# Phase A's last 768 tokens as a Strassen pair of halves in a kernel of attention and two gated MLPs

## The chip, the cores and the metric

One core of a Trainium2 chip runs the whole kernel. The metric is the device time of one execution in microseconds (us); lower is better. Several runs give a median, and one more execution is profiled.

## The reference, cut to what matters

Attention with a window of 32 positions (plain in four heads, with a step of 4 in the other four) runs over 4 sequences of 576 positions and 8 heads of 64. Its output, 2304 tokens by 512, goes through two MLPs one after the other.

```
x = attention(q, k, v)                      # 2304 tokens x 512
# phase A: d_ff 1536
a = x @ w_a;  b = x @ w_b
x1 = (a * b) @ w_out
# phase B: d_ff 2048
h = x1 @ w_in
g = maximum(h, 0) + alpha * minimum(h, 0)
out = g @ w_out2
```

## The kernel before

The weights come as float64, and their words are turned on the chip into float32 (`float_of`: two ScalarE operations, two VectorE operations for a block of 128x512). Every float32 operand of a matmul is then split into a high and a low part (`split`: a copy to fp32r gives the high part, a subtraction the low one), and each product is three matmuls: high by high, high by low, low by high (`mm3`). The contraction runs over features, tokens are the moving columns.

Two large SBUF tensors, `rt` (fp32r) and `ft` (float32), are cut by hand into places and rings that are used again over the phases. The program is recorded in steps: `step` records one block of 12 matmuls, then lets each conversion on the `belt` go one stage further, then whatever was asked for with `at_step`. A scheduler then sets the order on each engine, so a step's place is only the order in which things were written down. All DMAs go out from SyncE's one queue (SP), in its order, and an instruction there that waits holds back those behind it.

Phase A goes over tokens in `TILES`: 512, 512, 512, 256 and 512. For each of 12 blocks f of 128 features a tile does 12 matmuls into `pa` (w_a), 12 into `pb` (w_b), multiplies the two, splits the product, and does 12 matmuls into the four banks `accA` (w_out). So a tile has 432 matmuls of the tile's width. Beside tile 0 the weights w_a, w_b (`in_wab`) and w_out (`in_wo`) are loaded and converted; w_out's parts are written to DRAM (`wod`) and loaded again for each later tile through `wo_ring`, which has two places. Beside tiles 0 to 2 the attention of the next sequence runs; the tiles 3 and 4 have none.

Phase B goes over three pairs of 384 tokens, and does h by Strassen's scheme (Winograd's form): tokens in two halves, features in two halves, seven products in place of eight. One group is two feature blocks, seven `product`s of 6 matmuls of 384 columns (L593), and between them slots for `task`s, each 12 matmuls into `accB`, with the splits of earlier gates. The seven weight factors of each group are formed by `convert_s` beside tiles 1 to 4, written to DRAM (`wsd`) and loaded through `ws_ring`, which has seven places. The 16 blocks of w_out2 (`w2o`) are converted from `start_of[4] + 21` on, one every 3.5 steps, so most of them beside phase B's first groups.

The lines that matter are L389 to L391 (the three matmuls of `mm3`), L593 (`product`), L262 (reload of `wod`), L505 (load of `wsd`), L182 (load of raw weights), L164 to L174 (`float_of`), L232 and L235 (`split`), L404, L405 (`split_x` at the turn of a tile), L496, L497 (`split_x1`, the seven inputs of the products), L658 and L604 (copies and additions that put Strassen's sums together).

Of the kernel before, what the change touches and what calls it, by code (L numbers as in the profile page):

```python
# [33 lines left out]
TILES = [(0, 512), (512, 512), (1024, 512), (1536, 256), (1792, 512)]  # L34

HT = 384
# [23 lines left out]
def tile_kernel(ctx: ExitStack, tc: tile.TileContext, qk, v, mask, wab, wo1, w2, alpha, out):  # L60
# [6 lines left out]
    wod = dram.tile([NFA, 128, 1024], F32, name="wod")  # L67
    wsd = dram.tile([NFB // 2, 7, 128, 512], F32, name="wsd")
# [33 lines left out]
    raw_b_ring = Ring(ft, 4096, 1024, 2)  # L102
# [9 lines left out]
    mk = cut(ft, a0 + 4648, 720).bitcast(BF16).rearrange("p (m k) -> p m k", m=5)  # L112

    xs = [cut(rt, 4096 + 1536 * i, 2, 2, HT) for i in range(7)]
    w2o = [cut(rt, 16384 + 1024 * f if f < 12 else 1024 * (f - 12), 2, 512) for f in range(NFB)]
    gq_ring = Ring(rt, 28672, 2 * HT, 3)
    ws_ring = Ring(rt, 30976, 512, 7)
    ws_ring.places = ws_ring.places[3:] + ws_ring.places[:3]
# [120 lines left out]
    def job_w(k, f, j):  # L239
# [5 lines left out]
        queue.append((k, convert(wab[f, j], dest)))  # L245

    def job_o(k, f):
# [4 lines left out]
        def then():  # L252
            nc.sync.dma_start(out=wod[f], in_=wo[0, f].rearrange("p h n -> p (h n)").bitcast(F32))
# [257 lines left out]
    start_of = [n_start + 3 * NFA * t + t for t in range(n_tiles + 1)]  # L511
    for t in range(1, n_tiles):
        for f in range(NFA):
            reload_o(start_of[t] + 3 * f, t, f)
    for t in range(3):
        lag = (1, 2, 3, 4, 6)
        for i in range(NC * NG):
            Group(t + 1, i, start_of[t] + int(i * 2.64), lag, steady)
# [12 lines left out]
    def first_sums():  # L531
        srcs[0] = sums_x1()

    k = start_of[4]
    at_step(after, k + 2, begin_b)
    at_step(after, k + 8, first_sums)
    for j in range(7):
        at_step(after, k + 20 + 2 * j, lambda j=j: split_x1(j, srcs[0][j]))
    for j in range(7):
        at_step(after, k + 3 * NFA, lambda j=j: load_ws(j))  # L540
# [14 lines left out]
    for t, (t0, n) in enumerate(TILES):  # L555
        assert now[0] == start_of[t], (now[0], start_of[t])
        if t < 3:
            xn[t + 2] = cut(ft, 2048 * (t % 2), 4, 512)
        for f in range(NFA):
# [15 lines left out]
            if final and t + 1 < n_tiles:  # L575
# [11 lines left out]

    def product(i, acc, start):
        w, x = loaded.pop(0), xs[i]
# [15 lines left out]


    tasks = [(p, h, f) for p in range(NP) for h in range(2) for f in range(NFB)]
    ready, split_of, out_accs = {}, {}, []
    n_split = [0]

    def prepare():

        while n_split[0] < len(tasks) and len(split_of) < 3 and tasks[n_split[0]] in ready:
            task = tasks[n_split[0]]
            n_split[0] += 1
            g = ready.pop(task)
            q = gq_ring.next().rearrange("p (h n) -> p h n", h=2)
            split(q[:, 0], q[:, 1], g, nc.scalar, nc.vector)
            split_of[task] = q
            g_free.append(g)  # L620

    def task():
        if not tasks or tasks[0] not in split_of:
            return
        n_split[0] -= 1
        p, h, f = it = tasks.pop(0)
        q = split_of.pop(it)
        if f == 0:
            out_accs[:] = new_accs(f"B{p}{h}")
        expand(out_accs, w2o[f][:, 0], w2o[f][:, 1], q, HT, f == 0, f == NFB - 1)  # L630
        if f == NFB - 1:
            t0 = (2 * p + h) * HT
            for c in range(NC):
                def evacuate_b(acc=out_accs[c], c=c, t0=t0):
                    ev = ev_ring.next()
                    if c % 2:
                        nc.vector.tensor_copy(ev, acc[:, :HT])
                    else:
                        nc.scalar.copy(ev, acc[:, :HT])  # L639
                    nc.sync.dma_start(out=out[c, :, t0:t0 + HT], in_=ev)  # L640
                at_step(after, now[0], evacuate_b)

    def bslot(products=None, *then):

        for fn in then:
            at_step(after, now[0], fn)
        at_step(after, now[0], prepare)
        step(products)

    def group(p, i):  # L650
        f0, f1 = 2 * i, 2 * i + 1
        last = i == NFB // 2 - 1
        b0, b1, b2 = (ps.tile([128, 512], F32, tag=t, bufs=n, name=t) for t, n in (("at", 2), ("pa", 1), ("pb", 1)))
        s1, s2, s3 = s_places
        if (p, i) == (0, 7):
            g_free.extend(g_late)
        c11, c12, c21, c22 = (g_free.pop(0) for _ in range(4))
        copy = lambda out, acc: nc.scalar.copy(out, acc[:, :HT])  # L658

        def run(j, acc, start):  # L660
            def products():
                product(j, acc, start)
# [7 lines left out]
        bslot(run(0, b0, True), lambda: copy(s1, b0), lambda: refill(0))  # L670
# [78 lines left out]
```

## Time and profile before

| | us |
|---|---|
| median of 3 runs | 945.01 (943.8 to 948.72) |
| the profiled execution | 949.16 |
| its span, first to last instruction | 947.4 |
| PE busy in the span | 929.5 (98%) |
| VectorE (DVE), ScalarE (ACT), GpSimd (POOL) busy | 537.7, 385.7, 64.8 |

Matmuls are pipelined and their ends are modelled, so PE's busy time says where it had work, not that it was at its peak. Where PE runs without a wait, the time of a stretch divided by the matmuls that started in it is what one costs.

### The profile page before, as it was taken

The numbers are of one execution on the slowest core, as the hardware profiler recorded it, in microseconds if no ns is written. First come the engines' busy times: TensorE is split into PE (matmuls) and PEld (weight loads), VectorE is DVE, ScalarE is ACT, GpSimd is POOL, SyncE is SP. The second block draws the span as 40 slices with busy tenths as digits, with TensorE's granted clock in tenths as the row PEclk, the third lists the DMA queues.
The fourth block names the chain that finished last, engine by engine and source line by source line (L and its number), as shares of the span: only waits on it lengthen the run. The fifth ranks groups of instructions, "written<-read, shape, count | busy, mean of one in ns | idle before, by whom it ended". The sixth has DMA issues, their size and how long they took to land.

```text
span 947.4 us, 15065 instructions
## 1 busy us (share of the span) xinstructions
PE 929.5 (98%) x5641; PEld 811.2 (86%) x5644; DVE 537.7 (57%) x1116; ACT 385.7 (41%) x908; POOL 64.8 (7%) x70
## 2 busy tenths in 40 slices
PE   8899999999999999999999999899999999999997
PEld 5577777777787777799888879899999999999997
DVE  5689986534445353453524349868746485546442
ACT  5588884523344343433522336524222242222221
POOL 0000000200203030303500000000000000000000
PEclk9799999999999999999999999999999999999999
DMA  7568863534436343477735358756545435344200
GB/s 206 167 221 290 284 232 134 195 126 161 151 121 221 125 173 99 159 280 250 245 130 177 109 174 315 246 152 196 175 119 150 122 112 156 112 140 134 72 34 34
DMA packets 71401, 158.65 MB, mean 167 GB/s; under 512 B 8097, under 2 KB 22689, under 8 KB 71329
## 3 DMA queue, kind: packets, MB, share of 16 engines
q1 hardware_dynamic: 71328, 157.70, 50.8%
q8 instruction: 45, 0.74, 0.3%
q14 instruction: 28, 0.22, 0.1%
HBM read 127.25 MB, written 30.41 MB: 166 GB/s over the span
## 4 chain that ended last, share of the span: by engine, by line
PE 89%; DMA 5%; DVE 2%; ACT 1%; issue 1%; SPq 1%; POOL 0%; ACTq 0%; DVEq 0%; POOLq 0%
PE at L593 7%; PE accB L391 6%; PE accB L390 6%; PE accB L389 6%; PE accA L389 5%; PE pa L389 5%; PE pb L389 5%; PE accA L390 5%; PE accA L391 5%; PE pb L391 5%; PE pa L391 5%; PE pb L390 5%; PE pa L390 5%; PE pb L593 4%; PE pa L593 4%; PE sp L306 3%
## 5 line engine op out<-in xcount | busy, mean ns | idle before, releaser
L232 ACT CAST rt<-ft 128x512 fp32r<-128x512 f32 (+2 forms) x240 | 132.1, 558 | 279.6 <-PE accB L391 168.9
L235 DVE TENSOR_TENSOR rt<-ft,rt 128x512 fp32r<-128x512 f32 (+2 forms) x208 | 129.9, 626 | 128.1 <-ACT rt L232 126.4
L390 PE MATMUL accB<-rt 128*128 128x384 f32 x384 | 128.4, 334 | 0.0
L391 PE MATMUL accB<-rt 128*128 128x384 f32 x384 | 128.0, 334 | 0.0
L389 PE MATMUL accB<-rt 128*128 128x384 f32 x384 | 125.8, 334 | 0.4 <-ACT ft L639 0.4
L593 PE MATMUL at<-rt 128*128 128x384 f32 x432 | 89.0, 336 | 3.8 <-DMA rt<-wsd 2.7
L389 PE MATMUL accA<-rt 128*128 128x512 f32 (+1 forms) x240 | 91.2, 383 | 1.2 <-DMA rt<-wod 1.2
L389 PE MATMUL pa<-rt 128*128 128x512 f32 (+1 forms) x236 | 90.9, 385 | 0.5 <-ACT rt L404 0.4
L389 PE MATMUL pb<-rt 128*128 128x512 f32 (+1 forms) x236 | 90.0, 381 | 0.0
L572 DVE TENSOR_TENSOR ft<-ft,pb 128x512 f32<-128x512 f32 (+1 forms) x59 | 37.2, 630 | 92.6 <-PE pb L391 84.9
L390 PE MATMUL pa<-rt 128*128 128x512 f32 (+1 forms) x236 | 87.8, 372 | 1.2 <-DVE rt L405 1.2
L390 PE MATMUL accA<-rt 128*128 128x512 f32 (+1 forms) x240 | 88.7, 370 | 0.2 <-DVE rt L235 0.2
L391 PE MATMUL accA<-rt 128*128 128x512 f32 (+1 forms) x240 | 88.4, 369 | 0.0
L391 PE MATMUL pb<-rt 128*128 128x512 f32 (+1 forms) x236 | 88.2, 374 | 0.0
L391 PE MATMUL pa<-rt 128*128 128x512 f32 (+1 forms) x236 | 87.9, 373 | 0.0
L390 PE MATMUL pb<-rt 128*128 128x512 f32 (+1 forms) x236 | 87.8, 372 | 0.0
L593 PEld LDWEIGHTS at<-rt 128*128 128x128 f32 x432 | 75.7, 188 | 5.8 <-DMA rt<-wsd 2.4
L389 PEld LDWEIGHTS accB<-rt 128*128 128x128 f32 x384 | 71.8, 188 | 0.7 <-ACT ft L639 0.7
L390 PEld LDWEIGHTS accB<-rt 128*128 128x128 f32 x384 | 72.1, 188 | 0.3 <-DVE rt L235 0.2
L391 PEld LDWEIGHTS accB<-rt 128*128 128x128 f32 x384 | 72.0, 188 | 0.0
L235 POOL TENSOR_TENSOR rt<-ft,rt 128x512 fp32r<-128x512 f32 (+1 forms) x32 | 40.1, 1265 | 406.0 <-ACT rt L232 399.4
L327 ACT ACTIVATE ft<-ft 128x96 f32<-128x96 f32 x144 | 52.5, 366 | 33.2 <-DVE ft L322 32.9
(68 smaller groups left out, 1489.3 us busy)
## 6 DMA issues: line engine op xcount, KB each, us to landing
rt<-wsd SPq DMA_DIRECT2D x168, 256.0 KB, 2.9
rt<-wod SPq DMA_DIRECT2D x48, 512.0 KB, 3.5
ft<-in_w SPq DMA_DIRECT2D x32, 512.0 KB, 4.6
wsd<-rt SPq DMA_DIRECT2D x56, 256.0 KB, 2.7
ft<-in_wab SPq DMA_DIRECT2D x24, 512.0 KB, 4.8
ft<-in_qk SPq DMA_DIRECT2D x48, 208.0 KB, 3.0
ft<-in_v SPq DMA_DIRECT2D x48, 144.0 KB, 3.3
ft<-in_wo SPq DMA_DIRECT2D x12, 512.0 KB, 5.0
```

Source lines behind the costliest of these rows:

```text
L232: hi_eng.copy(hi, x)
L235: lo_eng.tensor_tensor(out=lo, in0=x, in1=hi.bitcast(F32), op=ALU.subtract)
L306: nc.tensor.matmul(self.sp[half, s * KT:(s + 1) * KT], lhsT=tq[half, s * QT:(s + 1) * QT], rhs=tq[half, GS * QT + s * QT:GS * QT + s * QT ...
L327: nc.scalar.activation(self.et[:, s], self.st[:, s], AF.Exp, bias=self.sm[:, 0, s:s + 1], accum_out=self.sm[:, 1, s:s + 1])
L389: nc.tensor.matmul(acc, lhsT=wh, rhs=rh, start=first, stop=False)
L390: nc.tensor.matmul(acc, lhsT=wh, rhs=rl, start=False, stop=False)
L391: nc.tensor.matmul(acc, lhsT=wl, rhs=rh, start=False, stop=last)
L572: at_step(after, k + 1, lambda g=g, pb=pb: nc.vector.tensor_tensor(out=g, in0=g, in1=pb[:, :n], op=ALU.mult))
L593: nc.tensor.matmul(acc[:, :HT], lhsT=a, rhs=x[:, b, c], start=start and c == k == 0, stop=c == 1 and k == 2, skip_group_check=not start,)
```

## The change

Phase A's tiles 3 and 4 (256 and 512 tokens) become one pair of halves of 384 tokens, done as phase B does its pairs. For each feature block f the seven products give w_a's and w_b's outputs of both halves (c11, c21 for the first half, c12, c22 for the second); `times` multiplies them; the first half's 12 tasks run in the groups, the second half's products are kept (`a_kept`) and its 12 tasks run after the groups, in `finish`.

The weights' seven factors are not loaded ready-made as in phase B. Each converted w_a and w_b block is written as float32 to DRAM beside tile 0 (`wad`, 24 writes of 256 KB), is loaded again (512 KB for a block f), and `form` makes the next group's factors in SBUF while a group runs: four ScalarE copies, four VectorE subtractions for the low parts, two GpSimd and two VectorE operations. `convert_s` now starts every 9 steps in place of 16, so all eight run beside tiles 1 and 2. The attention groups beside tile 2 start every 2.3 steps in place of 2.64. The w2o conversions start at the first step of `finish`, one every 3 steps, and the first seven `wsd` loads are asked for in the middle of the pair. The class `Second` holds what were `prepare`, `task`, `evacuate_b` and `bslot`, now for both phases; many places in `rt` and `ft` are moved.

```
-TILES = [(0, 512), (512, 512), (1024, 512), (1536, 256), (1792, 512)]
+TILES = [(0, 512), (512, 512), (1024, 512), (1536, 768)]
+N_PLAIN = 3
...
+    fac_ring = Ring(rt, 14848, 7 * 512, 2)
+    fw_ring = Ring(ft, 0, 1024, 2)
+    ga_ring = Ring(rt, 0, 2 * HT, 3)
...
+        def then(x):
+            nc.sync.dma_start(out=wad[f, :, j * 512:(j + 1) * 512], in_=x)
+
+        queue.append((k, convert(wab[f, j], dest, then)))
...
-        queue.append((start_of[1] + 2 + 16 * i, convert_s(i)))
+        queue.append((start_of[1] + 2 + 9 * i, convert_s(i)))
     for f in range(NFB):
         queue.append((
-            start_of[4] + 21 + 7 * f // 2,
+            rest + 1 + 3 * f,
...
+    def load_f(f):
+        if f < NFA:
+            fw[f] = w = fw_ring.next()
+            nc.sync.dma_start(out=w, in_=wad[f])
+
+    def form(f):
...
+        out(0, 0, 2)
+        out(3, 2, 1)
+        yield
+        nc.gpsimd.tensor_tensor(out=q[3], in0=q[2], in1=q[3], op=ALU.add)
+        nc.gpsimd.tensor_tensor(out=q[2], in0=q[0], in1=q[2], op=ALU.subtract)
+        nc.vector.tensor_tensor(out=q[0], in0=q[3], in1=q[0], op=ALU.subtract)
+        nc.vector.tensor_tensor(out=q[1], in0=q[1], in1=q[0], op=ALU.subtract)
+        yield
+        out(0, 3, 2)
+        yield
+        out(2, 5, 2)
+        load_f(f + 2)
+        yield
...
+    at_step(after, k + 32, lambda: sums_a.extend(sums(xn[N_PLAIN])))
     for j in range(7):
-        at_step(after, k + 3 * NFA, lambda j=j: load_ws(j))
+        at_step(after, k + 33 + j // 2, lambda j=j: split_x1(j, sums_a[j]))
...
+    def weights_a(f):
+        w = wo_pair.pop(0)
+        at_step(after, now[0], lambda: load_o(n_o[0]) or n_o.__setitem__(0, n_o[0] + 1))
+        return w
...
+        sec.slot(run(0, b0, True), lambda: copy(s1, b0), more, refill(0))
+        sec.slot(run(1, b1, True), lambda: add(c11, s1, b1), refill(1))
+        sec.slot(run(2, b0, False), lambda: copy(s2, b0), more, refill(2))
+        sec.slot(run(3, b2, True), refill(3))
+        sec.slot(run(4, b0, False), lambda: copy(s3, b0), more, refill(4))
+        b3 = ps.tile([128, 512], F32, tag="pa", name="pa")
+        sec.slot(run(5, b3, True), lambda: add(c22, s3, b2), lambda: add(c21, s3, b3), refill(5))
+        sec.slot(sec.task, lambda: times(c11, c21, 0), more)
+        sec.slot(run(6, b2, False), lambda: add(c12, s2, b2), lambda: times(c12, c22, 1), refill(6))
+    sec.finish()
```

What this makes of the engines' orders is shown at three places. The first is ScalarE (ACT) beside the last tokens. Before, in the last tile, it copies `pa` out (L568), splits a product (L232) and prepares phase B's inputs (L496):

```order
L568 COPY ft<-pa 128x512
L496 CAST rt<-ft 128x768
L232 CAST rt<-ft 128x512
L568 COPY ft<-pa 128x512
L232 CAST rt<-ft 128x512
```

Now one group of the pair has, in this order, the copy of the first sum out of PSUM (L669), the high parts of the first two factors, the copies of the second and third sum, the high part of one factor (128x256), of the task's input (128x384), and of the last four factors in two casts:

```order
L669 COPY ft<-at 128x384
L241 CAST rt<-ft 128x2x256
L669 COPY ft<-at 128x384 x2
L241 CAST rt<-ft 128x256
L241 CAST rt<-ft 128x384
L241 CAST rt<-ft 128x2x256 x2
```

So the last four factors of the next group are cast right ahead of that group's first copy, behind GpSimd's and VectorE's part of `form`.

The second place is the end of phase A. Before, SP has ahead of phase B the reloads of `wod` and the first loads of `wsd` and of raw w_out2 (`in_w`):

```order
L262 DMA rt<-wod 128x1024 x3
L482 DMA ft<-x1d 128x4x768
L262 DMA rt<-wod 128x1024
L182 DMA ft<-in_w 128x512
```

Now, in `finish`, SP has loads of `wod` (L590), of `wsd` (L517) and of `in_w` (L191) in turn:

```order
L590 DMA rt<-wod 128x1024 x2
L517 DMA rt<-wsd 128x512 x3
L590 DMA rt<-wod 128x1024
L191 DMA ft<-in_w 128x512
L590 DMA rt<-wod 128x1024
L517 DMA rt<-wsd 128x512 x2
```

PE, at the same place, has between two tasks of the second half (12 matmuls into `accA`, L401 to L403) some matmuls of phase B's first products (L655):

```order
L401 MATMUL accA_3_4778<-rt 128x384
L402 MATMUL accA_3_4778<-rt 128x384
L403 MATMUL accA_3_4778<-rt 128x384
L655 MATMUL pa<-rt 128x384 x3
L655 MATMUL pb<-rt 128x384 x3
L401 MATMUL accA_0_4775<-rt 128x384
```

So the tasks of `finish` do not stand back to back: phase B's products, 6 matmuls at most places, have been moved in between.

The third place is SP beside the start of tile 0. Before, the sixth block of w_a and w_b is loaded right behind the fifth:

```order
L182 DMA ft<-in_wab 128x512
L278 DMA ft<-in_v 96x384
L182 DMA ft<-in_wab 128x512
L182 DMA ft<-in_wo 128x512
L278 DMA ft<-in_v 96x384
L182 DMA ft<-in_wo 128x512
```

Now two writes of `wad` (L255) stand ahead of it:

```order
L191 DMA ft<-in_wab 128x512
L290 DMA ft<-in_v 96x384
L255 DMA wad<-ft 128x512
L290 DMA ft<-in_v 96x384
L191 DMA ft<-in_wo 128x512
L255 DMA wad<-ft 128x512
L191 DMA ft<-in_wab 128x512
L191 DMA ft<-in_wo 128x512
```

So the sixth load (the second L191 of `in_wab` here) now comes behind the write of the fifth converted block.

## Rows read from the trace of the kernel before

**Rows 1.** The page: the chain that ended last, share of the span by engine.
```profile
PE 89%; DMA 5%; DVE 2%; ACT 1%; issue 1%; SPq 1%; POOL 0%; ACTq 0%; DVEq 0%; POOLq 0%
```

**Rows 2.** Windows, PE alone: stretch, us, busy (matmuls), granted clock, DMA share, GB/s.
```profile
466.00:556.00 90.00, 90.00 (x399) 1.00 0.39 138
...
406.00:424.00 18.00, 18.00 (x152) 1.00 0.73 253
...
735.00:845.00 110.00, 110.00 (x637) 1.00 0.44 125
```

**Rows 3.** Timeline of ACT: the copies that follow tile 2's and the last tile's ends.
```profile
404.09 0.59 ACT L427 COPY ft<-accA 128x512 f32<-128x512 f32 x1 [2.39 <-PE accA L391]
...
558.07 0.59 ACT L427 COPY ft<-accA 128x512 f32<-128x512 f32 x1 [0.77 <-PE accA L391]
```

**Rows 4.** Waits of PE, 401 to 465 us: total us, times, longest.
```profile
PE pa L390 <- DVE rt L405: 1.2, 1, 1.2
```

**Rows 5.** Windows: stretch, us, PE, PEld, DVE, ACT, POOL busy (count), clock, DMA.
```profile
60.00:150.00 90.00, 90.00 (x580) 69.05 (x579) 81.09 (x177) 72.69 (x172) 0.00 (x0) 1.00 0.77 266
...
285.00:400.00 115.00, 115.00 (x727) 89.49 (x727) 50.64 (x120) 44.66 (x130) 23.17 (x24) 1.00 0.46 155
...
560.00:600.00 40.00, 37.95 (x209) 35.56 (x207) 32.64 (x64) 21.27 (x41) 0.00 (x0) 1.00 0.89 311
600.00:645.00 45.00, 43.13 (x243) 42.12 (x244) 32.52 (x67) 14.63 (x29) 0.00 (x0) 1.00 0.58 173
```

**Rows 6.** Waits of PE, 556 to 735 us: total us, times, longest.
```profile
PE at L593 <- DMA rt<-wsd: 2.7, 2, 2.1
```

**Rows 7.** Groups by form: shapes, count, busy us, mean ns of one, idle before.
```profile
L232 ACT CAST rt<-ft 128x512 fp32r<-128x512 f32 x124 | 75.2, 617 | 75.3 <-DVE ft L572 41.6 <-POOL ft L224 16.6 <-DVE ft L174 12.3
L235 DVE TENSOR_TENSOR rt<-ft,rt 128x512 fp32r<-128x512 f32 x100 | 70.4, 706 | 28.2 <-ACT rt L232 27.7
...
L658 ACT COPY ft<-at 128x384 f32<-128x384 f32 x72 | 34.6, 480 | 50.8 <-PE at L593 50.5
...
L604 DVE TENSOR_TENSOR ft<-ft,pb 128x384 f32<-128x384 f32 x48 | 26.5, 552 | 16.0 <-ACT ft L658 15.7 <-PE pb L593 0.2
...
L497 DVE TENSOR_TENSOR rt<-ft,rt 128x768 fp32r<-128x768 f32 x21 | 20.7, 1007 | 18.4 <-PE pb L390 8.7 <-PE pa L390 6.2 <-PE pa L391 2.7
...
L235 DVE TENSOR_TENSOR rt<-ft,rt 128x256 fp32r<-128x256 f32 x12 | 6.2, 514 | 3.6 <-ACT rt L232 3.6
L222 POOL TENSOR_TENSOR ft<-ft 128x256 f32<-128x256 f32 x8 | 6.0, 752 | 0.6
...
L487 DVE TENSOR_TENSOR ft<-ft 128x768 f32<-128x768 f32 x12 | 11.4, 953 | 4.1 <-DMA ft<-x1d 4.0
```

**Rows 8.** Timeline in phase B: a product of six matmuls and ACT's copy of it.
```profile
577.84 1.20 PE L593 MATMUL at<-rt 128*128 128x384 f32 x6
...
579.07 0.48 ACT L658 COPY ft<-at 128x384 f32<-128x384 f32 x1
```

**Rows 9.** DMA issues, median us to landing: all, 410 to 460, 59 to 64 us.
```profile
rt<-wod SPq DMA_DIRECT2D x48, 512.0 KB, 3.5
...
rt<-wod SPq DMA_DIRECT2D x11, 512.0 KB, 4.7
...
ft<-in_wo SPq DMA_DIRECT2D x1, 512.0 KB, 8.3
```

**Rows 10.** Line L235 on POOL: durations ns min/median/max, first and last start.
```profile
L235 POOL TENSOR_TENSOR rt<-ft,rt x32: 732/1294/2017, 180.4 to 471.9; 128x512 fp32r<-128x512 f32 x24, 128x256 fp32r<-128x256 f32 x8
```

**Rows 11.** Timeline of tile 0: two loads, conversions on DVE, a use on PE.
```profile
45.79 0.42 SPq L182 DMA_DIRECT2D ft<-in_wab  x1
...
52.53 1.28 DVE L174 SCALAR_TENSOR_TENSOR ft<-ft 128x512 uint32<-128x512 uint32 x2
...
68.67 0.68 DVE L174 SCALAR_TENSOR_TENSOR ft<-ft 128x512 uint32<-128x512 uint32 x1
...
71.17 0.50 PE L389 MATMUL pa<-rt 128*128 128x512 f32 x1
```

More of the change, by code (lines that the diff above doesn't have):

```diff
@@ L604, in add @@
         nc.vector.tensor_tensor(out=out, in0=x, in1=acc[:, :HT], op=ALU.add)
[L607 to L648, printed above, removed]
+    def copy(out, acc):
+        nc.scalar.copy(out, acc[:, :HT])
+    class Second:
+        def __init__(self, key, tasks, nf, parts, free, evs, weights, dst, first):
+            self.key, self.tasks, self.nf, self.parts, self.free = key, tasks, nf, parts, free
+            self.evs, self.weights, self.dst, self.first = evs, weights, dst, first
+            self.ready, self.split_of, self.accs, self.n = {}, {}, [], 0
+        def prepare(self):
+            while self.n < len(self.tasks) and len(self.split_of) < 3 and self.tasks[self.n] in self.ready:
+                it = self.tasks[self.n]
+                self.n += 1
+                g = self.ready.pop(it)
+                q = self.parts.next().rearrange("p (h n) -> p h n", h=2)
+                split(q[:, 0], q[:, 1], g, nc.scalar, nc.vector)
+                self.split_of[it] = q
+                self.free.append(g)
+        def task(self):
+            if not self.tasks or self.tasks[0] not in self.split_of:
+                return
+            self.n -= 1
+            p, h, f = it = self.tasks.pop(0)
+            q = self.split_of.pop(it)
+            if f == 0:
+                self.accs = new_accs(f"{self.key}{p}{h}")
+            w = self.weights(f)
+            expand(self.accs, w[:, 0], w[:, 1], q, HT, f == 0, f == self.nf - 1)
+            if f == self.nf - 1:
+                for c in range(NC):
+                    at_step(after, now[0], lambda c=c, acc=self.accs[c]: self.evacuate(
+                        acc, c, self.first + (2 * p + h) * HT))
+        def evacuate(self, acc, c, t0):
+            ev = self.evs.next()[:, :HT]
+            if c % 2:
+                nc.vector.tensor_copy(ev, acc[:, :HT])
+            else:
+                nc.scalar.copy(ev, acc[:, :HT])
+            nc.sync.dma_start(out=self.dst[c, :, t0:t0 + HT], in_=ev)
+        def slot(self, products=None, *then):
+            for fn in then:
+                at_step(after, now[0], fn)
+            at_step(after, now[0], self.prepare)
+            step(products)
+        def finish(self):
+            while self.tasks:
+                self.slot(self.task)
@@ new lines, in tile_kernel, with times @@
+    for f in range(NFA):
+        b0, b1, b2 = banks()
+        s1, s2, s3 = s_places
+        c11, c21, c22 = (a_free.pop(0) for _ in range(3))
+        c12 = a_kept.pop(0)
+        ws = factors.pop(f)
+        job = form(f + 1) if f + 1 < NFA else iter(())
+        more = lambda job=job: next(job, None)
+        run = lambda j, acc, start: lambda: product(ws[j], xs[j], acc, start)
+        refill = lambda j: lambda: split_x1(j, srcs[0][j]) if f == NFA - 1 else None
+        def times(a, b, h):
+            nc.vector.tensor_tensor(out=a, in0=a, in1=b, op=ALU.mult)
+            sec.ready[0, h, f] = a
+            a_free.append(b)
+        sec.slot(run(0, b0, True), lambda: copy(s1, b0), more, refill(0))
[7 more added lines that the diff above has]
+        sec.slot(run(6, b2, False), lambda: add(c12, s2, b2), lambda: times(c12, c22, 1), refill(6))
@@ L650, in group @@
+    sec.finish()
+    sec = Second("B", [(p, h, f) for p in range(NP) for h in range(2) for f in range(NFB)], NFB, gq_ring, g_free,
+                 ev_ring, lambda f: w2o[f], out, 0)
     def group(p, i):
@@ L690, in tile_kernel @@
             group(p, i)
-    while tasks:
-        bslot(task)
+    sec.finish()
     while after:
```

118 lines of the change are left out of this document (74 added, 44 removed).

## The prediction

> **What bounds the kernel now.** I read the page first: the chain that ended last is 89% PE [rows 1], so PE's time is what the change must shorten. Then PE alone in three stretches without attention [rows 2], where it has no idle time: the time over the matmuls that started in it (two less than the count, which reach in from before) is what one costs. That is 90.0/397 = 0.2267 us at 512 columns, 18.0/150 = 0.120 at 256, 110.0/635 = 0.1732 at 384, all at the full granted clock. A matmul thus costs its columns at 2.4 GHz plus about 32 columns more. Third, the stage that the change replaces: from the first copy behind tile 2 to the first copy behind the last tile 558.07 - 404.09 = 154.0 us [rows 3], of which its 864 matmuls fill 432 x 0.120 + 432 x 0.2267 = 149.8. The other 4.2 are waits at the narrow tile and at the turns, the largest single one for the split inputs of the last tile [rows 4]. Last, phase B's start: from 560 to 645 us some 448 matmuls of 384 columns (452 less those that reach in) take 85.0 us where 77.6 would do, so 7.4 are lost. There the DMAs run at 0.89 of their time and 311 GB/s, VectorE is busy 82% [rows 5], and PE's longest wait is for `wsd` [rows 6].
>
> **Matmuls.** The pair has 12 blocks with 7 products of 6 matmuls and 2 tasks of 12, together 12 x 66 = 792 of 384 columns: 792 x 0.1732 = 137.2 us. Against 149.8 that is **-12.5**. The 4.2 us of waits belong to a narrow tile and a turn that are gone: **-4.2**.
>
> **The turn into the pair.** `sums` and `split_x1` replace the `split_x` of two tiles. Behind the last attention group PE still has 72 matmuls of 512 columns, 16.3 us. VectorE has in that time four subtractions of 0.95, seven of 1.01 (the low parts), two multiplications and three splits at about 0.7 each, and 0.7 for `form`: 15.1 us [rows 7]. It just fits, and the products need the seven inputs one after the other, 1.04 us apart. I take **0**; without the cover up to +3.
>
> **The pair's groups.** One group is 54 matmuls, 9.36 us. VectorE has four additions and two multiplications at 0.55, low parts of 3 x 0.71 + 0.51, two 256-wide operations at 0.51 and the task's low part at 0.55: 7.5 us. ScalarE has three copies at 0.48, three casts at 0.62 and two of about 0.5: 4.3. So neither is the bound by its sum; the order may be. The third copy can start when product 4 is done, as in phase B 1.23 us after its start [rows 8], so 5.39 us into the group. From there, with the durations of [rows 7]: copy to 5.87, two VectorE additions (0.55 each) to 6.98, the low part of the last single factor (0.51) to 7.49, two GpSimd operations (0.75 each) to 8.99. VectorE's two operations and the task's split between them end at 9.82, ScalarE's cast (0.62) at 10.44. VectorE has the low parts of the other pair, the addition into c12 and the low parts of this pair still to do: 9.82 + 0.71 + 0.55 + 0.71 = 11.79. The next group's third product needs that low part in its third matmul, at 9.36 + 2.08 + 0.35 = 11.79. So the chain fits with nothing to spare, or with a little where short operations overlap. It can cost from 0 to 0.5 us a group, 0 to 5.5 in all; I take **+1**, as durations back to back overlap slightly.
>
> A rule speaks against this part. The Trainium skill, "GPSIMD Engine Reference", section "Key points", says that GpSimd shares its SBUF interfaces with VectorE and contends with VectorE instructions that have two SBUF inputs. Nearly all of VectorE's work here is of that kind. The rows agree that it can happen: the split on GpSimd took from 0.73 to 2.02 us at the same line, median 1.29 [rows 10], while the 256-wide additions stayed at 0.75. By the rule the two GpSimd operations would be slower, and the chain would miss by that much; rival C below prices it.
>
> **The finish.** 13 tasks are left when the groups end, and each needs 512 KB of `wod` from a ring of two places. The load for task n+2 can start only when task n has ended. PE's order has 6 matmuls of phase B's products between two tasks, so the load has 1.04 + 2.08 + 1.04 = 4.16 us. If it takes L, a pair of tasks loses L - 4.16, and 11 loads lose 5.5 times that. The median of all reloads is 3.5 us (nothing lost); in the stretch with the most traffic beside reloads it is 4.7 (+3.0), and in a burst at tile 0 a 512 KB load took 8.3 us (+22.8) [rows 9]. Traffic decides: from phase B's first product to the last task of A PE has 280 matmuls, 48.5 us, and the queue has 11 `wod` (5.8 MB), 18 `wsd` (4.7), 6 raw blocks (3.1), 2.4 of x1: 15.9 MB, 328 GB/s, where the saturated stretch gave 311 [rows 5]. That alone is 2.6 us. The row at 4.7 is nearest; I take **+4**, from 0 to +10 (L = 6).
>
> The Trainium skill, "DMA: Bandwidth & Descriptors", section "Anatomy of one DMA — SWDGE (gpsimd) path", gives 2.0 us plus the bytes at 436 GB/s for one DMA on another queue than this one. That makes an estimate of 3.2 us for 512 KB, nothing lost here, and a sum 4 us lower. The rows at 4.7 and 8.3 under traffic speak against relying on it.
>
> **Phase B's start.** The 7.4 us lost before had to do with `wsd` arriving as phase B began and with the conversions of w2o. Now seven `wsd` are there beforehand, and some 6 of 16 conversions are done by the end of A. The rest still come beside groups that are short of matmuls (66 in place of 90), at one every 3 steps in place of 3.5, and keep VectorE nearly full. I put +3.5 (0 to +7) in place of 7.4: **-3.9**.
>
> **Tile 0.** 24 writes of 256 KB, 6.3 MB, come on top of 266 GB/s from 60 to 150 us [rows 5], about 70 GB/s more, which is close to the highest rates seen. And SP is held: the load of the sixth block, out at 45.8 us, now comes behind the write of the fifth, which waits for a conversion that started at 52.5 [rows 11]. The ninth conversion is just in time even now (68.7 for a use at 71.2); later ones have more lead. I take **+1**, 0 to +5.
>
> **Tiles 1 and 2.** The denser `convert_s` costs nothing: PE had no idle time there, ACT was busy 39% and VectorE 44% [rows 5]. Without that cover each late split would stand in PE's way.
>
> **Sum.** -12.5 - 4.2 + 0 + 1 + 4 - 3.9 + 1 = -14.6. Against the profiled execution of 949.2 that is 934.6. The median of the runs, 945.0, lies 4.2 below that execution; I apply the difference to it: **930.4 us**.
>
> **Rivals.** A, the forecast: 926 to 935. B: the loads of `wod` take 6.3 us under the finish's traffic: 5.5 x 2.1 = 11.8 in place of 4, 938. For it speaks that SP's queue mixes them with raw loads that wait for conversions. C: the groups wait for their factors 0.6 us each, 6.6 in place of 1: 936; for it the chain without slack, against it that copies and additions overlap. By the rule on GpSimd the time would be this one. D: the finish is hidden and phase B starts without loss: -8 more, 922. E, slower than before: the reloads take 8.3 us as in tile 0's burst, +22.8 in place of +4: 949.2. It decides from L = 7.5 us on, where the loss is 18.6 and the whole gain is gone. Against it: the burst had six loads out at once, the finish has two or three. F: the change gives its gain back in tile 0, conversions late by 7 us in place of 1: 936; against it the lead of the later conversions.
>
> **Chances.** A 0.54, B 0.15, C 0.08, D 0.10, F 0.04, two of B, C and F together (about 942) 0.06, E 0.03. Faster by over 0.5%, which is about what a measurement of this kernel can tell from no change, is below 940.3: A to D and F less a tail of 0.04, 0.87. Within 0.5% (to 949.7) lie the doubles and most of the tail, 0.09; slower 0.04, E's worse end and a little for what I have not seen. The range leaves out E, the upper half of the doubles and the lower half of D: 922 to 943.
>
> **What would show it.** Between the first copy behind tile 2 and the last task of A there should be 792 matmuls of 384 columns at 0.173 us. A group at 9.4 us says that the factor chain holds; at 10 us and with PE waiting for VectorE's line 244, C. In the finish the waits for `wod` should total about 4 us; 12 or more says B, 20 E. Phase B's first 80 us should lose some 4 us. In tile 0 the waits of PE for conversions should stay below 2 us. I am wrong if the groups or tile 0 lose more than 5 us, or the finish more than 10.

## The result and the profile after

The changed kernel takes 955.18 us (median of 9 runs, 952.16 to 962.07), the kernel before 947.59 beside it: the ratio is 1.0084, interval 1.0059 to 1.011. It is slower; 930.4 had been forecast. The profiled execution took 957.92 us, 8.8 more than the one before.

Where the time went shows when PE's matmuls are counted off. A tile ends here where its 432nd matmul of 512 columns starts, and the rest runs from there to PE's last matmul:

| us | tile 0 | tile 1 | tile 2 | rest | sum |
|---|---|---|---|---|---|
| before | 164.5 | 120.6 | 120.6 | 536.6 | 942.3 |
| after | 157.3 | 138.5 | 120.8 | 534.5 | 951.1 |
| difference | -7.2 | +17.9 | +0.2 | -2.1 | +8.8 |

So the largest item is tile 1, to whose stretch the change adds only the denser conversions (and moves some places), and the stage that the change was made for gave 2.1. The chain that ended last is now 74% PE, where it was 89% [rows 1], and the loads of raw weights (`in_w`) alone have 6% of it:

```profile
PE 74%; DMA 12%; DVE 6%; ACT 4%; POOL 2%; issue 2%; SPq 1%; DVEq 0%; ACTq 0%; POOLq 0%
```

Windows of after (us, busy and count of PE, PEld, DVE, ACT, POOL, then clock and DMA), in the place of the row of 115 us of [rows 5]:

```profile
165.00:220.00 55.00, 54.23 (x342) 41.62 (x340) 28.88 (x57) 27.21 (x74) 20.89 (x22) 1.00 0.65 214
220.00:297.00 77.00, 66.20 (x379) 51.15 (x380) 35.56 (x79) 35.66 (x88) 28.36 (x28) 0.91 0.68 231
297.00:412.00 115.00, 115.00 (x723) 89.80 (x724) 62.90 (x132) 47.75 (x132) 16.77 (x18) 1.00 0.47 158
```

Between 220 and 297 us PE stands idle for 10.8 us, and the mean clock of 0.91 over 77 us comes from 13.6 us at half speed. Of these, 1.6 lie in a pause, and in the other 12.0 some 6.0 are lost. With 0.8 us idle between 165 and 220 us that is 17.6 of the 17.9. Yet ScalarE and VectorE are each busy only 46% there. The waits of after from 155 to 300 us (total, times, longest) name what the busy share hides:

```profile
ACT ft L173 <- DMA ft<-in_w: 27.4, 11, 7.3
ACT rt L241 <- POOL ft L233: 21.8, 6, 4.4
PE accA L401 <- ACT rt L241: 4.5, 1, 4.5
PE ap L368 <- ACT ft L360: 3.3, 2, 2.1
PE tp L355 <- DVE ft L328: 2.5, 1, 2.5
```

SP's queue in the same stretch:

```profile
SPq L223 <- POOL rt L244: 62.9, 16, 7.4
```

In the kernel before, in tile 1 (163 to 284 us), the same three were:

```profile
ACT ft L164 <- DMA ft<-in_w: 3.2, 4, 1.8
ACT rt L232 <- POOL ft L224: 3.2, 2, 1.8
SPq L214 <- POOL rt L235: 14.1, 8, 5.0
```

How they hang together is seen in 20 us of the timeline of after (start, duration, idle before and its end):

```profile
264.41 0.44 SPq L274 DMA_DIRECT2D rt<-wod  x1
266.82 0.66 ACT L173 ACTIVATE ft<-ft 128x512 f32<-128x512 f32 x1 [7.29 <-DMA ft<-in_w]
...
271.50 2.25 POOL L244 TENSOR_TENSOR rt<-ft,rt 128x512 fp32r<-128x512 f32 x2 [11.19 <-ACT rt L241]
272.87 6.51 SPq L223 DMA_DIRECT2D wsd<-rt  x4
...
277.04 1.66 ACT L241 CAST rt<-ft 128x512 fp32r<-128x512 f32 x3 [4.41 <-POOL ft L233]
277.74 2.99 POOL L244 TENSOR_TENSOR rt<-ft,rt 128x512 fp32r<-128x512 f32 x2 [0.73 <-ACT rt L241]
...
280.44 0.38 SPq L191 DMA_DIRECT2D ft<-in_w  x1
...
285.37 0.66 ACT L173 ACTIVATE ft<-ft 128x512 f32<-128x512 f32 x1 [6.29 <-DMA ft<-in_w]
285.93 0.57 ACT L632 COPY ft<-pa 128x512 f32<-128x512 f32 x1
...
288.96 0.68 DVE L636 TENSOR_TENSOR ft<-ft,pb 128x512 f32<-128x512 f32 x1
289.99 0.60 ACT L241 CAST rt<-ft 128x512 fp32r<-128x512 f32 x1
290.65 0.80 PE L401 MATMUL accA<-rt 128*128 128x512 f32 x1 [4.53 <-ACT rt L241]
...
291.96 0.63 PE L403 MATMUL accA<-rt 128*128 128x512 f32 x1
```

It is a circle. ScalarE waits 7.29 us for a raw block, so its casts are late; GpSimd's low parts wait for those; the writes of `wsd` wait for GpSimd, and SP, in order, issues nothing from 264.85 to 272.87. The raw blocks for the next job come behind those writes (280.44), land late, and ScalarE waits again. Behind its wait stands the copy of `pa` (285.93), behind that VectorE's multiplication and the split's cast, and PE waits 4.53 us; then its matmuls take 0.63 us each (0.39 at full clock) until 296.

### The profile page after: what moved, and what is told of

Its sections match the earlier page's. It is cut to its first block, busy times and chain, and to the rows that moved or that the text cites. A ratio compares the mean times of both kernels' runs of the same rounds, so it can differ in the third digit from the quotient of the medians.

```text
span 956.0 us, 15231 instructions
## 1 busy us (share of the span) xinstructions
PE 921.6 (96%) x5569; PEld 818.1 (86%) x5572; DVE 592.5 (62%) x1229; ACT 415.3 (43%) x967; POOL 84.0 (9%) x94
## 4 chain that ended last, share of the span: by engine, by line
PE 74%; DMA 12%; DVE 6%; ACT 4%; POOL 2%; issue 2%; SPq 1%; DVEq 0%; ACTq 0%; POOLq 0%
PE at L655 10%; PE pb L655 7%; PE pa L655 7%; PE accB L401 6%; PE accB L403 6%; PE accB L402 6%; DMA ft<-in_w 6%; PE accA L401 4%; PE accA L402 4%; PE accA L403 4%; PE pb L401 2%; PE pa L401 2%; PE pb L403 2%; PE pb L402 2%; PE pa L402 2%; PE pa L403 2%
## 5 line engine op out<-in xcount | busy, mean ns | idle before, releaser
L244 DVE TENSOR_TENSOR rt<-ft,rt 128x512 fp32r<-128x512 f32 (+1 forms) x256 | 158.6, 623 | 125.1 <-ACT rt L241 117.0
L655 PE MATMUL at<-rt 128*128 128x384 f32 x648 | 132.7, 336 | 0.6 <-ACT ft L669 0.6
L401 PE MATMUL accB<-rt 128*128 128x384 f32 x384 | 125.6, 335 | 4.3 <-DVE ft L708 1.5
L403 PE MATMUL accB<-rt 128*128 128x384 f32 x384 | 127.9, 334 | 0.0
L655 PEld LDWEIGHTS at<-rt 128*128 128x128 f32 x648 | 113.4, 188 | 4.2 <-ACT ft L669 4.1
L401 PE MATMUL accA<-rt 128*128 128x512 f32 (+1 forms) x240 | 93.1, 391 | 7.0 <-ACT rt L241 4.5
L655 PE MATMUL pb<-rt 128*128 128x384 f32 x432 | 88.9, 338 | 4.3 <-DVE ft L666 4.3
L403 PE MATMUL accA<-rt 128*128 128x512 f32 (+1 forms) x240 | 90.9, 379 | 0.0
L655 PE MATMUL pa<-rt 128*128 128x384 f32 x432 | 88.3, 336 | 0.0
L669 ACT COPY ft<-at 128x384 f32<-128x384 f32 x108 | 51.7, 480 | 71.1 <-PE at L655 68.3
L655 PEld LDWEIGHTS pb<-rt 128*128 128x128 f32 x432 | 76.3, 189 | 6.7 <-DVE ft L666 3.8
L180 DVE SCALAR_TENSOR_TENSOR ft<-ft 128x512 uint32<-128x512 uint32 x68 | 47.6, 700 | 49.5 <-ACT ft L176 49.2
L655 PEld LDWEIGHTS pa<-rt 128*128 128x128 f32 x432 | 76.5, 189 | 0.3 <-DVE ft L666 0.3
L401 PEld LDWEIGHTS accB<-rt 128*128 128x128 f32 x384 | 71.7, 188 | 5.3 <-DVE ft L708 1.8
L403 PEld LDWEIGHTS accB<-rt 128*128 128x128 f32 x384 | 72.0, 188 | 0.0
L173 ACT ACTIVATE ft<-ft 128x512 f32<-128x512 f32 x68 | 45.5, 669 | 46.6 <-DMA ft<-in_w 42.9
L244 POOL TENSOR_TENSOR rt<-ft,rt 128x512 fp32r<-128x512 f32 (+1 forms) x32 | 38.0, 1197 | 262.3 <-ACT rt L241 230.3
```

The lines of the kernel that those rows point to most:

```text
L173: nc.scalar.activation(f, high.bitcast(F32), AF.Abs, scale=2.0 ** -112)
L180: nc.vector.scalar_tensor_tensor(out=fi, in0=fi, scalar=3, in1=low, op0=ALU.logical_shift_left, op1=ALU.bitwise_or)
L244: lo_eng.tensor_tensor(out=lo, in0=x, in1=hi.bitcast(F32), op=ALU.subtract)
L401: nc.tensor.matmul(acc, lhsT=wh, rhs=rh, start=first, stop=False)
L403: nc.tensor.matmul(acc, lhsT=wl, rhs=rh, start=False, stop=last)
L655: nc.tensor.matmul(acc[:, :HT], lhsT=a, rhs=x[:, b, c], start=start and c == k == 0, stop=c == 1 and k == 2, skip_group_check=not start,)
```

## The experiments

Eighteen profiles can be set side by side. "Groups", "finish" and "B" are the time lost in the pair's groups, from there to A's last task, and from that to the end: first start to last, less 0.17325 us for each matmul of 384 columns (before, B lost 8.0). The expectations count a tile from the first copy behind one tile to that behind the next, which gives 120.4 before and 136.9 after for tile 1.

| run | ratio to before (95%) | tile 0 | tile 1 | tile 2 | groups, finish, B |
|---|---|---|---|---|---|
| after | 1.0084 (1.0059, 1.011) | 157.3 | 138.5 | 120.8 | 3.7, 9.0, 10.0 |
| e1 | 1.012 (1.008, 1.0161) | 161.5 | 136.9 | 120.6 | |
| e2 | 1.0046 (1.0018, 1.0075) | 158.0 | 122.5 | 136.2 | 3.6, 7.5, 9.5 |
| e3 | 0.988 (0.9838, 0.9921) | 156.9 | 120.6 | 124.9 | 3.6, 4.9, 8.9 |
| e4 | 0.9956 (0.9931, 0.998) | 158.6 | 126.9 | 121.3 | 4.0, 3.3, 8.5 |
| e5 | 0.9845 (0.9816, 0.9874) | 157.5 | 120.6 | 120.7 | 4.3, 4.7, 6.4 |
| e6 | 0.9832 (0.9808, 0.9857) | 158.1 | 120.6 | 122.9 | 0.3, 6.0, 7.9 |
| e7 | 0.9955 (0.993, 0.998) | 162.2 | 120.6 | 120.6 | |
| e8 | 0.9848 (0.9819, 0.9877) | 158.1 | 120.6 | 120.7 | 3.7, 5.3, 9.7 |
| e9 | 0.995 (0.9931, 0.9969) | 161.5 | 120.6 | 120.6 | |
| e10 | 0.9817 (0.9792, 0.9843) | 156.6 | 120.6 | 120.7 | 0.5, 4.4, 8.0 |
| e11 | 0.983 (0.9806, 0.9854) | 160.3 | 120.6 | 120.7 | 0.5, 2.8, 9.3 |
| e12 | 0.9831 (0.9803, 0.9859) | 157.5 | 120.6 | 120.7 | 0.5, 3.4, 10.6 |
| e13 | 0.9843 (0.9827, 0.986) | 156.8 | 120.6 | 120.7 | 0.4, 4.5, 13.3 |
| e14 | 0.981 (0.979, 0.9829) | 160.2 | 120.6 | 120.7 | 0.4, 4.2, 6.8 |
| e15 | 0.9817 (0.9798, 0.9836) | 158.0 | 120.6 | 121.8 | 0.6, 7.1, 6.4 |
| e16 | 0.9815 (0.9787, 0.9842) | 156.9 | 120.6 | 120.7 | 0.4, 5.3, 7.2 |
| e17 | 0.9823 (0.9788, 0.9859) | 160.4 | 120.6 | 120.8 | 0.6, 4.3, 6.3 |

**e1: the density alone.**

```
-        queue.append((start_of[1] + 2 + 16 * i, convert_s(i)))
+        queue.append((start_of[1] + 2 + 9 * i, convert_s(i)))
```

> The kernel before, with one number of the change: convert_s every 9 steps in place of 16. Theory 1 (the density alone makes the loss): tile 1, 120.4 us in the kernel before, takes 132 to 137, tile 2 121 to 124, and the kernel is 10 to 17 us slower than before. Theory 2 (the loss comes from what else moved, the places of the raw blocks and of the tile inputs, or the reads of the turn): tile 1 stays at 120 to 122 and the time within 0.5% of before.

Tile 1 takes 136.9 us (135.1 as the expectation counts) and the kernel 1.2% more. One number in the old kernel makes 16.3 of the 17.9 us that tile 1 lost, with the same waits (163 to 298 us):

```profile
ACT ft L164 <- DMA ft<-in_w: 25.9, 12, 7.0
SPq L214 <- POOL rt L235: 60.2, 15, 7.3
```

Theory 1 holds. Tile 2, where the conversions are as dense, loses nothing in the table (122.2 as the expectation counts). Why the circle does not close there was not tried.

**e2: the writes from GpSimd's queue.**

```
-                nc.sync.dma_start(out=wsd[i, place], ...
+                nc.gpsimd.dma_start(out=wsd[i, place], ...
```

> The changed kernel with the writes of wsd issued by GpSimd's queue in place of SP's. Theory 1a (the loads of raw weights are held in SP's queue behind writes that wait for GpSimd's low parts, and ScalarE then waits for them): SP's 62.9 us of waits at these writes go, ScalarE's 27.4 us of waits for in_w fall under 8, tile 1 falls from 136.9 to 122 to 128 us, the time by 8 to 14 us. Theory 1b (ScalarE waits for GpSimd itself, and the density is too much whatever SP does): tile 1 stays at 132 to 137 and the time moves by less than 4 us.

ScalarE's waits for `in_w` fall to 5.7 us and tile 1 to 122.5, as 1a has it. But the time falls by only 0.4%, since tile 2 now loses 15.6, in pauses of 1.5, 2.9 and 5.1 us with half clock beside each. The longest is a wait for a split at the turn to the pair: GpSimd spends 0.5 us on each issue, the last job runs into the turn, and VectorE does the pair's subtractions ahead of the multiplication that the split needs. Which of these costs how much was not tried apart. The expectation was right on the mechanism and wrong on the time.

**e3: the raw blocks earlier.** The places are free when `float_of` has read them; the next load is asked for there instead of at the next job's start.

```
+        if i + 1 < NFB // 2:
+            raws_of[i + 1] = load_s(i + 1)
         q = [f[:, h * 256:(h + 1) * 256] for f in fs for h in range(2)]
```

> The changed kernel with the next pair of raw blocks loaded as soon as the two places are free, about 4 steps earlier, and the same number of conversions. Theory 1a (late raw blocks are what ScalarE waits for): its waits for in_w fall from 27.4 us to under 10, tile 1 to 124 to 130 us, the time by 6 to 12. Theory 1b: the earlier loads are held behind the same writes or ScalarE waits for GpSimd in their place; tile 1 stays over 132 us.

Tile 1 is back at 120.6, nothing lost, and the time falls by 18 us, more than expected. The waits in tile 1 of this kernel (158 to 278 us):

```profile
ACT rt L248 <- POOL ft L240: 12.3, 4, 3.9
ACT ft L173 <- DMA ft<-in_w: 5.2, 6, 2.0
```

SP still waits 34.6 us for GpSimd there, but that no longer reaches PE. Tile 2 shows a loss of 4 at its end: waits of 1.7 and 0.3 us, with half clock behind the first.

**e4: convert_s's low parts on VectorE.**

```
-            split(w[:, :, 0], w[:, :, 1], y, nc.scalar, nc.gpsimd)
+            split(w[:, :, 0], w[:, :, 1], y, nc.scalar, nc.vector)
```

> The changed kernel with convert_s's low parts on VectorE in place of GpSimd (32 subtractions, 0.5 to 0.7 us each; the four additions stay on GpSimd). Theory 1 in both forms (GpSimd's slow low parts hold SP's writes and ScalarE's copies): tile 1 falls from 136.9 to 121 to 127 us and the time by 9 to 15 us. Rival (VectorE is then too late with the attention's and the tile's operations): tile 1 stays over 131 us.

Tile 1 takes 126.9: both of ScalarE's waits are halved (13.7 and 11.3 us), SP's writes wait 36.8 us for VectorE in place of 62.9 for GpSimd, and one wait of PE, of 3.7 us, is left. GpSimd is one link of the circle, not all of it.

**e7: the old kernel, dense, with early loads.** e1's and e3's edits together.

> The kernel before with convert_s every 9 steps (as e1) and the next pair of raw blocks loaded as soon as the places are free (as e3). Theory (late raw blocks are the whole loss of the density): tile 1 returns to 120 to 123 us and the time to within 0.5% of the kernel before. Rival (the density costs by itself, through GpSimd's low parts in front of ScalarE): tile 1 stays at 127 or more and the time is 0.7% or more above the kernel before.

Tile 1 takes 120.6: the density costs nothing once the blocks come in time. The kernel is even 0.45% faster than before: the rest takes 533.0 us, 536.6 before. The conversions then end ahead of the narrow tile; that this is why was not tried apart.

**e9: where tile 0's 7 us came from.** The old kernel plus the change's 24 writes, which nobody reads.

```
+        def then(x):
+            nc.sync.dma_start(out=wad[f, :, j * 512:(j + 1) * 512], in_=x)
```

> The kernel before, with the 24 writes of converted w_a and w_b blocks to DRAM of the change added, and nothing else; nobody reads them. Theory (the writes change the order in which the scheduler puts ScalarE's work in tile 0, the exps come ahead of a conversion, PE's stall of 2.6 us at 32 us shrinks to 1 and the half clock behind it goes): tile 0 ends at 153 to 156 us instead of 163 and the kernel is 0.6 to 1.0% faster than before. Rival (the changed kernel's better tile 0 comes from something else, and 6.3 MB of writes cost as forecast): tile 0 ends at 162 to 168 us, the same time as before or up to 0.5% slower.

6.3 MB of useless writes make the kernel 0.5% faster. From its first matmul of 512 columns tile 0 takes 132.2 us, 138.8 before and 131.7 after. ScalarE in the kernel before, and PE behind it:

```profile
29.82 0.65 ACT L164 ACTIVATE ft<-ft 128x512 f32<-128x512 f32 x1 [1.61 <-DMA ft<-in_wab]
30.38 0.64 ACT L167 ACTIVATE ft<-ft 128x512 f32<-128x512 uint32 x1
30.92 0.36 ACT L327 ACTIVATE ft<-ft 128x96 f32<-128x96 f32 x1
...
32.50 0.57 PE L356 MATMUL ap<-ft 96*64 96x64 f32 x12 [2.61 <-ACT ft L348]
```

and after:

```profile
29.26 0.38 ACT L339 ACTIVATE ft<-ft 128x96 f32<-128x96 f32 x1 [1.13 <-DVE ft L334]
...
30.86 0.57 PE L368 MATMUL ap<-ft 96*64 96x64 f32 x12 [1.03 <-ACT ft L360]
```

In after and in e9 alike, the scheduler, with the writes in its list, put the exps ahead of the conversion that in the kernel before had waited 1.61 us for its block. PE's longest wait for ScalarE's work in tile 0 shrinks from 2.61 us to about 1, and in e9 it is 0.9. So the order and the shorter pause are as the theory has them; the half clock is not. The windows from 30 to 45 us (columns as in the rows of windows above, the clock is the third from the end), before and then e9:

```profile
30.00:45.00 15.00, 12.50 (x76) 7.89 (x78) 7.16 (x28) 8.36 (x28) 0.00 (x0) 0.61 0.44 138
30.00:45.00 15.00, 13.51 (x109) 8.81 (x109) 10.47 (x39) 9.53 (x31) 0.00 (x0) 0.88 0.76 225
```

The kernel before was at half clock from 33.3 to 47.0 us, but e9 was too, from 23.4 to 33.6. And e1 and e7, which have the old tile 0 without the writes, have the long pause with little or no half clock behind it (3.4 us in e1, none in e7, whose clock from 30 to 45 us is 1.00). Their waits, e1 first:

```profile
PE ap L356 <- ACT ft L348: 3.1, 3, 2.5
PE ap L363 <- ACT ft L355: 2.6, 2, 2.5
```

From the first matmul of 512 columns their tile 0 takes 136.2 and 134.9 us. So the writes are worth 2.7 to 4.0 us against these two, and how much of the 6.6 against the profiled execution of before is the order and how much its clock stays open. Over all runs the mean granted clock is 0.997 in e9's 12 and 0.994 in the 17 of the kernel before beside it. Over spans of some 942 us that is about 2.5 of the 5.5 us between the medians. By the expectation's count tile 0 ends at 160.0 us, later than the theory's 153 to 156 and earlier than the rival's 162 to 168; 0.5% came where 0.6 to 1.0 was expected. In this execution the first matmul came 3.6 us later than in the kernel before.

**e5: the sums in their place.** On e3.

```
-        nc.sync.dma_start(out=xb, ...
+        tc.keep_in_program_order(nc.sync.dma_start(out=xb, ...
-        sub(ts[0], b12, b11)
+        tc.keep_in_program_order(sub(ts[0], b12, b11))
```

> The kernel of e3 with the load of phase B's next x1 and the first of its four subtractions held at their place in the written order, so that the scheduler can't put them ahead of the additions that PE waits for. Theory (VectorE's order at the turn into phase B is what the pb waits come from): PE's 4.0 us of waits of pb for the additions and the 2 us at accB go mostly, 3 to 5 us less than e3. Rival (they only move into the pair's groups, whose VectorE has no time for 3.8 us more, or the conversions of the output weights are the bound there): within 2 us of e3.

What it undoes is this, in the timeline of after: a subtraction for the next x1, which the program asks for behind phase B's fifth group, stands, in its first, ahead of the addition that PE needs.

```profile
542.09 0.96 DVE L499 TENSOR_TENSOR ft<-ft 128x768 f32<-128x768 f32 x1 [5.22 <-DMA ft<-x1d]
542.97 0.55 DVE L666 TENSOR_TENSOR ft<-ft,pb 128x384 f32<-128x384 f32 x1
...
543.66 0.41 PE L655 MATMUL pb<-rt 128*128 128x384 f32 x1 [2.53 <-DVE ft L666]
```

The wait goes, finish and B lose 11.1 in place of 13.8, and tile 2's end no longer loses its 4. The medians, 935.52 and 937.23, are closer than that, and the intervals overlap: the profile shows the theory's waits gone, the times do not decide between theory and rival.

**e6: form on VectorE.** On e3; the two GpSimd operations of `form` become VectorE's.

> The kernel of e3 with form's two GpSimd operations on VectorE. Theory (ScalarE's cast of the last factors stands ahead of its copy of the next group's first product, since the chain over GpSimd is late; it costs 0.28 us a group): a group of the pair falls from 9.64 to 9.36 us, 3 us less in all than e3. Rival (VectorE then is the late engine): a group stays at 9.6 or more.

The groups lose 0.3 us in place of 3.6, as the theory has it. In the kernel after, ScalarE's cast of the last factors stood ahead of the copy that frees a bank:

```profile
452.91 0.74 POOL L575 TENSOR_TENSOR ft<-ft 128x256 f32<-128x256 f32 x1
453.68 0.43 DVE L576 TENSOR_TENSOR ft<-ft 128x256 f32<-128x256 f32 x1 [1.45 <-POOL ft L575]
453.68 0.62 ACT L241 CAST rt<-ft 128x512 fp32r<-128x512 f32 x1 [0.90 <-POOL ft L575]
454.49 0.42 DVE L577 TENSOR_TENSOR ft<-ft 128x256 f32<-128x256 f32 x1
455.00 0.63 ACT L241 CAST rt<-ft 128x512 fp32r<-128x512 f32 x1 [0.70 <-PE at L655]
455.52 0.47 ACT L669 COPY ft<-at 128x384 f32<-128x384 f32 x1
```

The second cast reads what VectorE's L577 writes, and that ended at 454.91, behind the chain over GpSimd. (The profile puts this wait down to PE, whose product 0 ended at 454.99, at almost the same moment.) So the copy of product 0 is 0.5 us late, and the third product starts at 456.05 in place of 455.87.

**e8, e10, e11, e12: combinations.** e8 is e3 with e4; e10 is e3, e5 and e6; e11 adds a third place for `wod` in the pair; e12 adds e4.

```
+    wo_p_ring.places.append(cut(rt, 3072, 1024))
```

> The kernel of e3 with convert_s's low parts on VectorE as well (e3 and e4 together). Theory (with the blocks early ScalarE's remaining waits for GpSimd do not reach PE in tile 1): within 2 us of e3. Rival (what is left in tile 1 and 2, 3 us each against the kernel before, is GpSimd's): 3 to 6 us less than e3.

> The changed kernel with the early loads (e3), the sums in place (e5) and form on VectorE (e6) together. Theory (three separate losses): gains add, a group of the pair 9.36 us, the time some 3 us below e3's and 0.3% below e5's and e6's, about 0.981 of the kernel before. Rival (VectorE, with both, becomes the late engine in the pair): no better than e5 or e6 alone, or a group over 9.5 us.

> As e10, with a third place for the reloaded output weights in the finish of phase A. Theory (a load into a ring of two places is exposed by what it takes beyond 4.16 us): PE's waits for wod, 3.0 us in e5, fall under 0.5, and the kernel is 2 to 3 us below e10. Rival (the conversions or the splits of the tasks are then as late): the same time as e10 within 1 us.

> As e11, with convert_s's low parts on VectorE as well (as e8). Theory (what was left of ScalarE's waits for GpSimd in tiles 1 and 2 no longer reaches PE): within 1.5 us of e11. Rival: 2 us or more below e11, from tile 2's end, or above it, if VectorE is late at the turn into the pair.

e8 is e3's time, as its theory has it: tile 2 no longer loses 4, and finish and B lose 1.2 more. e10 comes out about as its theory has it: 930.71 us, ratio 0.9817, with 0.5 us lost in the groups. e11's theory fails: 1.4 us of waits for `wod` are left where under 0.5 was expected, 1.6 us less are lost in the finish, B loses 1.3 more, and the time is no better. e12 changes nothing.

**e13 to e17: what is left in finish and B.** All on e10: e13 gives the low parts of the output weights to GpSimd, e14 spaces their conversions by 4 steps (`rest + 1 + 4 * f`), e15 leaves out their `float_of` (the weights, and so the output, are then not the reference's), e16 is e11 with e14, e17 is e11 with e15.

> The kernel of e10 with the low parts of the 16 output-weight blocks of phase B on GpSimd, which is idle there. Theory (VectorE, 86 to 92% busy behind the end of phase A, is the bound): the 7.2 us lost in phase B's first 80 us fall to 4 or less, and the time by 3 to 5 us. Rival (GpSimd's low parts take 1.3 us each and come later, or VectorE slows beside them, as the rule on shared interfaces has it): the same within 1.5 us, or worse.

> The kernel of e10 with the 16 conversions of output weights every 4 steps in place of 3. Theory (VectorE's bound by density): the loss behind the end of phase A is 2 to 4 us less. Rival (the tasks need the blocks as fast as they come, so that spreading them only moves the wait): the same within 1.5 us or 1 to 3 us more.

> The kernel of e10 with the raw words of the 16 output-weight blocks loaded but not turned into floats (two ScalarE and two VectorE operations each left out; the splits are made of what lies in the place), so the output is not the reference's. Theory (the conversions' work is the bound): the loss behind the end of phase A falls from 7 to 8 us to 3 or less. Rival (PE is short of work there for another reason, the additions, gates and splits of the groups): it stays over 5.

> The kernel of e10 with the third place for wod (e11) and the conversions every 4 steps (e14). Theory (two limits, both eased): the loss of finish and phase B together falls from 12.4 to 7 to 10 us, the time 2 to 5 below e10. Rival (VectorE's sum of work is the limit of the stretch, however it is placed): 11 us or more, the time as e10's within 1.5 us.

> The kernel of e11 (third place for wod) with the conversions' arithmetic left out as in e15, so the output is not the reference's. Theory (two limits of one stretch): with both away the loss of finish and phase B together is 6 us or less, half of what either leaves. Rival (something else, the loads of wsd or the evacuations, is the limit): 10 us or more.

e13 is worse by 5 in B, so its rival holds. Without the conversions' arithmetic (e15) VectorE is busy 50 to 63% from 557 to 600 us, where it was 86 to 92% in e10, and finish and B still lose 13.5 (12.4 in e10): B loses 1.6 less, the finish 2.7 more, where PE's waits for `wod` go from 2.6 to 4.7 us. With the third place as well (e17) 10.6 are left, so the rival holds: neither is the limit, nor are both. e14 and e16 are e10's time within the intervals. What costs these 10 us is not settled.

## Why the prediction was wrong

Term by term, in us of the profiled executions:

| term | forecast | measured |
|---|---|---|
| matmuls | -12.5 | -12.6 |
| waits of the narrow tile and its turn | -4.2 | -4.2 |
| turn into the pair | 0 | 0 |
| groups | +1 | +3.7 |
| finish | +4 | +9.0 |
| phase B's start | -3.9 | +2.0 |
| tile 0 | +1 | -7.2 |
| tiles 1 and 2 | 0 | +18.1 |
| sum | -14.6 | +8.8 |

The matmuls are 2952 of 384 columns at 0.17325, 511.4, against 149.8 + 2160 x 0.17325 = 524.0. The waits are 154.2 from tile 2's end to phase B's first matmul less 149.8, against 0.2 now.

**The step that failed** is "The denser `convert_s` costs nothing: PE had no idle time there, ACT was busy 39% and VectorE 44%". It read cover from busy shares. The shares rose only to 46%, and tile 1 lost 17.9 us. What counts on engines that work in order is what stands ahead of the instruction that is due: ScalarE spent 49 us of tile 1 blocked, on data (27.4) and on GpSimd (21.8), with the tile's copies and casts behind. The prediction's own last sentence on it, that without the cover each late split would stand in PE's way, is what came. e1 shows that this one number makes 16.3 of the 17.9, e3 and e7 that late raw blocks are the cause, e2 and e4 that the hold in SP's queue and GpSimd's low parts are links of the circle.

**Groups.** They lost 3.7 us in 12 groups, a little over half of rival C's 6.6, and since e6 removes it, the cause is the late chain over GpSimd, as C has it. But PE did not wait for factors (it has no wait for L244 there): its weight loads waited 3.8 us, in ten groups, for the copy (L669) that stands behind the cast. The chain was worked out to fit with nothing to spare, and one step of it was too short. It puts the end of VectorE's two operations and the split 0.83 us behind GpSimd's second operation (8.99 to 9.82); in the trace it is 1.26 (453.65 to 454.91), since VectorE's first operation overwrites what GpSimd's second reads and so starts only behind it.

**Finish.** The size was right only by its upper end, and the reason was another: `wod` cost 2.5 us in one wait (its loads landed in 4.0 us by median, where 4.7 had been taken), the order of VectorE 2.5, and each pause brought half clock after it (545 to 548.5 and 582.6 to 586 us, 1.7 lost in each). Rivals B and E, slow reloads, did not come.

**Phase B's start.** "I put +3.5 in place of 7.4" failed: the whole of phase B lost 10.0 against 8.0, its first 80 us 6.4 against 6.7. It had ascribed the old loss to `wsd` and the conversions. e15 and e17 show that in the changed kernel the conversions' arithmetic is not the main cause (4.7 are lost in these 80 us in both, 7.2 in e10); the loss of the old kernel was not taken apart.

**Tile 0.** Forecast +1 for traffic; in the profiled executions it gained 7.2. Part of it comes from an order that only the scheduler knew (e9), part from the 13.7 us at half clock that this execution of the kernel before had there: e1 and e7, with its tile 0, end it at 161.5 and 162.2 us, not at 164.5. This luck hid two fifths of the loss in tile 1.

With the three mends the change pays: e10 takes 930.71 us where the kernel before takes 948.96 beside it, and beats both kernels. That this is the number of the forecast is luck. In its profile tile 0 gives 7.9 us where +1 was forecast, and phase B, which lost 8.0 before, still loses 8.0.

## What to carry to other kernels

A busy share is no cover on an engine that works in order: ask for each added instruction what it can wait for, and what is queued behind it; above all where a load is issued behind writes that wait for the work that the load feeds. Ask for a load when its place is free, not when its job begins. Where a scheduler sets the order, compare stage by stage: an edit can gain or lose microseconds in a stage that it does not name.

## What the runs showed of the hardware

GpSimd and VectorE slow each other. Operations of VectorE by form from 508 to 640 us in e10, then in e13, where GpSimd did 16 low parts there:

```profile
L671 DVE SCALAR_TENSOR_TENSOR ft<-ft 128x384 f32<-128x384 f32 x31 | 17.2, 554 | 0.2
L670 DVE TENSOR_SCALAR ft<-ft,al 128x384 f32<-128x384 f32 x31 | 12.9, 416 | 0.1
L674 DVE TENSOR_TENSOR ft<-ft,pa 128x384 f32<-128x384 f32 x17 | 9.4, 551 | 0.9 <-PE pa L663 0.7
```

```profile
L251 POOL TENSOR_TENSOR rt<-ft,rt 128x512 fp32r<-128x512 f32 x16 | 21.8, 1365 | 208.0 <-ACT rt L248 208.0
L671 DVE SCALAR_TENSOR_TENSOR ft<-ft 128x384 f32<-128x384 f32 x29 | 19.2, 661 | 0.7
L670 DVE TENSOR_SCALAR ft<-ft,al 128x384 f32<-128x384 f32 x29 | 16.5, 570 | 0.3
L674 DVE TENSOR_TENSOR ft<-ft,pa 128x384 f32<-128x384 f32 x16 | 8.8, 549 | 0.5 <-PE pa L663 0.3
```

The gates went from 554 to 661 ns and from 416 to 570; the additions with an operand in PSUM stayed at 550. The other way round, in e2 GpSimd's operations of 256 columns (L230 to L233) took 0.74 to 0.81 us from 360 to 364 us and 1.34 to 1.39 us from 396 to 400, where VectorE did its 768-wide operations; one of those took 1.69 us, others 0.95. The spread in [rows 10] is in part that of two widths: 256 columns took 0.73 to 1.19 us there, 512 columns 1.27 to 2.02. The Trainium skill, "GPSIMD Engine Reference", section "1. Specifications", says that the SBUF interfaces are shared and that contention comes with two SBUF inputs or a two-port mode of VectorE. The rows agree for the operation with two tiles as input (L671). The one with one tile (L670) slowed most; whether it was in such a mode no row shows.

PE's granted clock fell to half (1.2 of 2.4 GHz) at pauses, but the length of a pause does not tell whether it does. In tile 1 of after it was at half for 3.4, 3.4 and 6.8 us at the pauses of 2.5, 2.1 and 4.5 us that ended at 223.6, 271.8 and 290.6 us. A pause of 1.5 us that ended at 300.2 us in e2 had 3.4 us of half clock behind it; pauses of 2.5 us that ended at 34.1 us in e7 and at 546.9 us in e15 had none. The 10.8 us of pauses between 220 and 297 us in after thus cost some 6 more.
